# Reordering VectorE, ScalarE and POOL around the first two pairs of chunks in an output stage

## The chip, the cores and the metric

One core of a Trainium2 chip runs the whole program. The metric is the device time of one launch in microseconds. Five engines matter: TensorE (PE, with its weight loads shown apart as PEld), VectorE (DVE), ScalarE (ACT), GpSimd (POOL) and the DMA queues, most of them issued from SyncE (SP).

## The reference

The input x is 2048 by 448. The result is `g * a + (1 - g) * b`, with g a sigmoid gate of one number per row. Branch a is linear attention with 16 heads of width 28: q, k and v are projections of x, `phi(t) = where(t > 0, t + 1, exp(t)) + 1e-6` is applied to q and k, and then

```
kv  = einsum("bhsd,bhse->bhde", pk, v)
num = einsum("bhqd,bhde->bhqe", pq, kv)
den = einsum("bhqd,bhd->bhq", pq, z)[..., None] + 1e-6      # z: pk summed over the rows
a   = (num / den) @ wo
```

Branch b is a long convolution of x plus a skip; the kernel computes it with running sums when its taps are flat enough and with a general routine otherwise. With these inputs the general routine isn't entered.

## The kernel before, in words

The 2048 rows are 16 chunks of 128. A first stage goes over the chunks, projects k and q of each, and sums the outer product of pk and x into four PSUM banks g. fp32 products are made of fp32r pieces: an operand is split into a high part (ScalarE copies it, which rounds) and a low part (VectorE or POOL subtracts the high part), and three products of high and low parts are summed.

Between the stages (lines 716 to 821) the four banks are copied to SBUF as gs, multiplied by the v weights (`kv_products`), masked per head, split (kvh, kvl) and multiplied by wo. This gives a matrix M of 448 by 448, of which `m_high` and `m_low` write the parts mh and ml, four blocks of rows j. The q projection of the last chunk, 11 products, is spread over this stretch as filler for PE: `q_run(n)` issues the next n of them.

The output stage works on chunks in pairs. For chunk c:

- `norm_a(c)` on POOL multiplies pq by z into one of three buffers `prod`; `norm_b(c)` on DVE reduces it per head into the PSUM tile `den`.
- `norm_d(c, n)` finishes n chunks: a DVE multiply (L605), a DVE reciprocal (L607), and a copy of the result to SBUF for POOL (L610), on ACT where it says `ACT.copy`.
- `norm_c(c)` scales pq by that: POOL (L621), DVE (L624), POOL (L628), into `room`.
- `turn_pe(c)` transposes it on PE (L633) into a PSUM bank, t0 for the even chunk of a pair, t1 for the odd one.
- `turn_even` splits t0: ACT writes the high part th (L640), DVE the low part tl (L641). `odd_high` and `odd_low` do so for t1 (L652, L659). The odd chunk's fourth block lies in the even chunk's bank: `odd_ends(c, i, t0)` copies it on ACT (L656, two copies each) out of partitions 0 to 63 of t0 (i = 0) and 64 to 127 (i = 1).
- `attend(c)` is 11 products of 448 columns on PE (L676) in the order high, low, high and so on: the first loads th[c] block 2, the second tl[c] block 2, the sixth multiplies ml block 0, the ninth ml block 1, and the last two the ends.
- `final_b(c)` on DVE adds the gated convolution to it (L681) and the row block is written out from SP; `final_c(c)` copies it on ACT (L687).

The order of every engine's queue is that of the program text: the tile pools are under `manual_schedule()`, so an engine runs its instructions in the order in which the Python lines issue them, and waits are put in where an instruction touches a tile that another engine touched before. Each engine works through its queue strictly from the front; only PE's weight loads stand beside its products.

What the steps of the prediction touch: the kv products (L755), the M rows (L739, L743), the copies of the ends of M (L810, L813, L820), the first pair's lines 797 to 821, and the loop's turn c = 2 at lines 845 to 871.

Of the kernel before, what the change touches and what calls it, by code (L numbers as in the profile page):

```python
# [7 lines left out]
F32 = mybir.dt.float32  # L8
# [3 lines left out]
ALU = mybir.AluOpType  # L12
# [10 lines left out]
J = 4  # L23
# [119 lines left out]
def gated_mix_kernel(ctx: ExitStack, tc: tile.TileContext, xin, wq_d, wvo_d, abc_d, ldt_d, dsk_d,  # L143
                     turn_d, cst_d, first_d, gin_d, out):
    nc = tc.nc
    PE, ACT, DVE, POOL, SP = nc.tensor, nc.scalar, nc.vector, nc.gpsimd, nc.sync
# [62 lines left out]
    o = 0  # L209
    for part in PARTS:  # L210
# [8 lines left out]
        o = e  # L219
# [102 lines left out]
    def pieces(c, wh, wl, n, tag, last=None):  # L322
        o = ps.tile([P, 512], F32, name=tag, tag=tag)
        h, l = ([xt[c][:, i + k * P:i + (k + 1) * P] for k in range(J)] for i in (0, NAT))
        hh, lh, hl = ([(a[k], w[:, k]) for k in range(J)] for a, w in ((h, wh), (l, wh), (h, wl)))
        hl = hl[1:]
        if last == "x":
            seq = hh + hl + lh
        else:
            seq = [p for k in range(J) for p in (hh[k], lh[k])] + hl  # L330
            if last and len(last) > 1:
                seq = [{"h": hh, "l": lh, "w": [None] + hl}[i[0]][int(i[1])] for i in last.split()]
            elif last == "w":
                seq = seq[2:6] + seq[8:9] + seq[6:8] + seq[9:] + seq[:2]

        def run(count):
            for _ in range(min(count, len(seq))):
                a, b = seq.pop(0)
                run.n += 1
                PE.matmul(o[:, :n], lhsT=a, rhs=b, start=run.n == 1, stop=not seq)  # L340
        run.n = 0
        return o, run
# [249 lines left out]
    pn, th, tl, pd, dn, dp = {}, {}, {}, {}, {}, []  # L592

    def norm_a(c):
        pd[c] = prod[:, c % 3]
        POOL.tensor_tensor(out=pd[c], in0=pq[:, c], in1=zb, op=ALU.mult)  # L596

    def norm_b(c):
        if not dp:
            dp.append(ps.tile([P, 512], F32, name="den", tag="v1")[:, :NC * H].rearrange("p (c h) -> p c h", c=NC))  # L600
        DVE.tensor_reduce(out=dp[0][:, c], in_=pd.pop(c).rearrange("p (h d) -> p h d", h=H), op=ALU.add, axis=AX.X)  # L601

    def norm_d(c, n, copy=DVE.tensor_copy):
        r = dp[0][:, c:c + n]
        DVE.scalar_tensor_tensor(out=r, in0=r, scalar=1e-6, in1=e1[:, c:c + n, None].to_broadcast([P, n, H]),  # L605
                                 op0=ALU.add, op1=ALU.mult)
        DVE.reciprocal(out=r, in_=r)  # L607
        if c % 2 == 0:
            dn[c // 2] = tp.tile([P, 4, H], F32, name="den", tag="den", bufs=3)
        copy(dn[c // 2][:, c % 2:c % 2 + n], r)  # L610
# [5 lines left out]
    def norm_c(c):  # L616
        n = pn[c] = rf[:, c % 4 * NAT:][:, :NAT].rearrange("p (j t) -> p j t", j=J)
        r = dn[c // 2][:, c % 2]
        a = pq[:, c, :3 * DJ].rearrange("p (j h d) -> p j h d", j=3, h=4)
        b = pq[:, c, 3 * DJ:].rearrange("p (h d) -> p h d", h=4)  # L620
        POOL.tensor_tensor(out=n[:, :3, :DJ].rearrange("p j (h d) -> p j h d", h=4), in0=a,  # L621
                           in1=r[:, :H - 4].rearrange("p (j h) -> p j h", j=3)[:, :, :, None].to_broadcast([P, 3, 4, DH]),
                           op=ALU.mult)
        DVE.tensor_tensor(out=n[:, :3, DJ:].rearrange("p j (h d) -> p h j d", h=4),  # L624
                          in0=b[:, :, :DS].rearrange("p h (j d) -> p h j d", j=3),
                          in1=dp[0][:, c, H - 4:, None, None].to_broadcast([P, 4, 3, DS // 3]), op=ALU.mult)
        ends = pn[c // 2 * 2][:, 3, c % 2 * DT:][:, :DT].rearrange("p (h d) -> p h d", h=4)
        POOL.tensor_tensor(out=ends, in0=b[:, :, DS:], in1=r[:, H - 4:, None].to_broadcast([P, 4, DH - DS]), op=ALU.mult)  # L628

    def turn_pe(c):  # L630
        o = p3.tile([P, 512], F32, name="tr", tag="tr")
        for j in range(4 - c % 2):
            PE.transpose(o[:, j * P:(j + 1) * P], pn[c][:, j], ident)  # L633
        return o

    def turn_even(c, o):
        t = xt_p.tile([P, 2, J, P], F32R, name="th", tag="t")
        th[c], tl[c] = t[:, 0], t[:, 1]
        ov = o.rearrange("p (j t) -> p j t", j=J)
        ACT.copy(th[c], ov)  # L640
        DVE.tensor_tensor(out=tl[c], in0=ov, in1=th[c].bitcast(F32), op=ALU.subtract)  # L641

    def turn_odd(c, o, oe):
        odd_high(c, o)
        odd_ends(c, 0, oe)
        odd_ends(c, 1, oe)
        odd_low(c, o)

    def odd_high(c, o):
        t = xt_p.tile([P, 2, J, P], F32R, name="th", tag="t")  # L650
        th[c], tl[c] = t[:, 0], t[:, 1]
        ACT.copy(th[c][:, :3], o[:, :3 * P].rearrange("p (j t) -> p j t", j=3))  # L652

    def odd_ends(c, i, oe):
        for half in (slice(0, DT), slice(DT, P)):
            ACT.copy((th, tl)[i][c][half, 3], oe[i * DT:(i + 1) * DT, 3 * P:])  # L656

    def odd_low(c, o):
        DVE.tensor_tensor(out=tl[c][:, :3], in0=o[:, :3 * P].rearrange("p (j t) -> p j t", j=3),  # L659
                          in1=th[c][:, :3].bitcast(F32), op=ALU.subtract)  # L660
# [4 lines left out]
    def attend(c, cuts):  # L665
        av[c] = []
        even = c // 2 * 2
        h, l, ends = th[c], tl[c], (th, tl)[c % 2][even + 1][:, 3]
        for i, (lo, hi) in enumerate(cuts):
            pool, tag = ((p3, "a"), (p3, "a"), (ps, "v0"), (ps, "k"))[(c + i) % 4]  # L670
            a = pool.tile([P, 512], F32, name="a", tag=tag)
            av[c].append((a, lo, hi))
            seq = [(u_[:, j], w_[:, j]) for j in (2, 0, 1) for u_, w_ in ((h, mh), (l, mh), (h, ml))]
            seq += [(ends, mh[:, 3]), (tl[even][:, 3], low_w3[c % 2])]
            for n, (u_, w_) in enumerate(seq):
                PE.matmul(a[:, lo:hi], lhsT=u_, rhs=w_[:, lo:hi], start=n == 0, stop=n == 10)  # L676

    def final_b(c):
        ot = tp.tile([P, D], F32, name="ot", tag="pkh")
        for a, lo, hi in av[c]:  # L680
            DVE.scalar_tensor_tensor(out=ot[:, lo:hi], in0=y[:, c, lo:hi], scalar=og[:, c:c + 1],  # L681
                                     in1=a[:, lo:hi], op0=ALU.mult, op1=ALU.add)
            (ACT if c == NC - 1 and hi == D else SP).dma_start(out=oview[c, :, lo:hi], in_=ot[:, lo:hi])

    def final_c(c):
        for a, lo, hi in av.pop(c):
            ACT.copy(pq[:, c, lo:hi], a[:, lo:hi])  # L687

    c = NC - 2
# [26 lines left out]
    for i in range(4):  # L716
        do_g(c + 1, (i,))
        ACT.copy(gs[i], g[i][:, :D])
        if i == 1:
            qo, q_run = pieces(c + 1, wqh, wql, D + 2, "q")  # L720
# [17 lines left out]
    def m_high(j, o):  # L738
        ACT.copy(mh[:DJ, j] if j < 3 else shl[:, 0], o[:DJ, :D])  # L739
# [10 lines left out]
    def kv_products(r):  # L750
        kvp = ps.tile([P, 512], F32, name="k", tag="k") if r else p3.tile([P, 512], F32, name="tr", tag="tr")
        for j in (2 * r, 2 * r + 1):
            js = slice(j * DJ, (j + 1) * DJ)
            for k in range(4):
                PE.matmul(kvp[:DJ, js], lhsT=wv[:, (k + 1) % 4, js], rhs=gs[k][:, js], start=k == 0, stop=k == 3)  # L755
        return kvp
# [17 lines left out]
    def kv_low(r, o):  # L774
        DVE.tensor_tensor(out=kvl[:, 2 * r:2 * r + 2], in0=o, in1=kvh[:, 2 * r:2 * r + 2].bitcast(F32), op=ALU.subtract)

    q_run(1)
    k1 = kv_products(1)
    k0 = kv_products(0)
    k1 = kv_split(1, k1)  # L780
# [16 lines left out]
    t0 = turn_pe(0)  # L797
    t1 = turn_pe(1)
    q_run(2)
    norm_a(4)  # L800
    turn_even(0, t0)
    odd_high(1, t1)
    norm_b(2)
    norm_b(3)
# [2 lines left out]
    o1 = m_products(1, ps, "v0")  # L807
    m_high(0, o0)
    m_high(1, o1)
    ACT.copy(mh[:DT, 3], shl[:DT, 0].bitcast(F32))  # L810
    odd_ends(1, 0, t0)
    norm_d(2, 2, ACT.copy)
    ACT.copy(low_w3[0][:DT], shl[:DT, 0].bitcast(F32))  # L813
    m_low(0, o0)
    m_low(1, o1)
# [25 lines left out]
    norm_b(4)  # L841
    norm_a(7)
    norm_b(5)
    norm_d(4, 2, ACT.copy)
    for c in range(2, NC, 2):
        more = c + 2 < NC
        final_b(c - 2)
        t0 = turn_pe(c)
        t1 = turn_pe(c + 1)
        if more:  # L850
            norm_c(c + 2)
        if c + 6 < NC:
            norm_a(c + 6)
        if c + 4 < NC:
            norm_b(c + 4)
        turn_even(c, t0)
        if more:
            norm_c(c + 3)
        if c + 6 < NC:
            norm_a(c + 7)  # L860
        turn_odd(c + 1, t1, t0)
        final_c(c - 2)
        attend(c - 1, ((0, D),))
        if c + 4 < NC:
            norm_b(c + 5)
            norm_d(c + 4, 2, ACT.copy)
        final_b(c - 1)
        final_c(c - 1)
        attend(c, ((0, D),))
        for _ in range({4: 1, 6: 2}.get(c, 0)):  # L870
            next(later, None)
# [92 lines left out]
```

## Time and profile before

| | |
|---|---|
| time, median of 3 runs | 168.16 us (168.1 to 168.77) |
| the profiled execution's own time | 168.38 us |
| its span | 166.4 us |
| PE busy | 161.1 us (97%) |
| PEld busy | 144.9 us (87%) |
| DVE busy | 116.1 us (70%) |
| ACT busy | 109.4 us (66%) |
| POOL busy | 104.9 us (63%) |

The span is that of the program's instructions; some 2 us lie around it. A PE product of 448 columns is recorded as about 0.36 us, but products overlap in the array, so the distance between two starts is the number that adds up. The stretch of the change goes from about 112 us (kv products) over 118 to 126 us (first pair) to 130 us (the pair of c = 2).

### The profile page before, as it was taken

What the parts mean: (1) busy time and instruction counts of PE and PEld (TensorE: products, weight loads), DVE (VectorE), ACT (ScalarE), POOL (GpSimd) and SP (SyncE); (2) the same over time, 40 slices, a digit from 0 to 9 for tenths busy, and PEclk for the clock granted to TensorE, in tenths of its full rate; (3) what the DMA queues carried; (4) which work ended last, traced back from release to release, by engine and by line L of the source; (5) the groups of instructions that cost most, each with busy time, mean ns of one, the idle gap of its engine ahead of it and who ended that gap; (6) DMA issues with size and microseconds to landing.
All of it is one profiled execution on the core that took longest, in us unless ns stands there. A gap on an engine that the chain in (4) does not pass through costs nothing.

```text
span 166.4 us, 2609 instructions
## 1 busy us (share of the span) xinstructions
PE 161.1 (97%) x835; PEld 144.9 (87%) x835; DVE 116.1 (70%) x243; ACT 109.4 (66%) x257; POOL 104.9 (63%) x116
## 2 busy tenths in 40 slices
PE   6999999999999999999999999999999999999991
PEld 2698999999999999999999999988987999999990
DVE  0837753685852879889885555898899979986441
ACT  3688668988486784766758966453856766676541
POOL 3073589678809449477295999749689998633000
PEclk9999999999999999999999999999999999999998
DMA  5999966687974330959988007997121221122222
GB/s 157 411 314 321 287 143 230 228 295 276 336 255 136 126 107 19 221 141 250 295 261 165 0 4 117 185 203 161 27 46 55 110 110 55 61 110 110 110 78 95
DMA packets 10783, 27.51 MB, mean 165 GB/s; under 512 B 1328, under 2 KB 6992, under 8 KB 10544
## 3 DMA queue, kind: packets, MB, share of 16 engines
q1 hardware_dynamic: 8992, 21.71, 39.1%
q0 software_dynamic: 1632, 5.51, 17.6%
q8 instruction: 7, 0.11, 0.3%
q10 hardware_dynamic: 144, 0.11, 0.2%
q14 instruction: 8, 0.07, 0.1%
HBM read 17.87 MB, written 3.67 MB: 129 GB/s over the span
## 4 chain that ended last, share of the span: by engine, by line
PE 87%; DVE 6%; DMA 2%; ACT 1%; issue 1%; ACTq 0%; DVEq 0%
PE g L416 21%; PE q L340 19%; PE a L676 19%; PE v L340 12%; PE k L340 11%; PE tr L633 3%; DMA y<-in 2%; DVE den L601 2%; PE k L755 1%; DVE wk L743 1%; DVE th L641 1%; DVE ot L681 1%; ACT kvh L772 0%; DVE shl L743 0%; ACT wk L466 0%
## 5 line engine op out<-in xcount | busy, mean ns | idle before, releaser
L676 PE MATMUL a<-wk,th 128*128 128x448 f32 (+1 forms) x178 | 37.4, 357 | 0.3 <-DVE th L641 0.3
L416 PE MATMUL g<-pkh,xn 128*128 128x448 f32 x112 | 35.7, 364 | 0.0
L676 PEld LDWEIGHTS a<-wk,th 128*128 128x128 f32 x178 | 31.3, 188 | 2.9 <-DVE th L641 0.7
L237 POOL TENSOR_TENSOR xt<-xr,xt 128x512 fp32r<-128x512 f32 x14 | 18.2, 1298 | 19.8 <-ACT xt L241 19.8
L340 PE MATMUL q<-wqh,xt 128*128 128x450 f32 x120 | 27.8, 367 | 0.0
L237 POOL TENSOR_TENSOR xn<-xr,xn 128x448 fp32r<-128x448 f32 x16 | 19.6, 1228 | 10.1 <-ACT xn L247 10.1
L340 PEld LDWEIGHTS q<-wqh,xt 128*128 128x128 f32 x120 | 22.5, 189 | 1.8
L416 PE MATMUL g<-pkl,xn 128*128 128x448 f32 x64 | 23.3, 364 | 0.0
L416 PEld LDWEIGHTS g<-pkh,xn 128*128 128x128 f32 x112 | 21.1, 188 | 2.3
L596 POOL TENSOR_TENSOR prod<-pq,zb 128x448 f32<-128x448 f32 x16 | 18.3, 1154 | 4.5 <-ACT zb L709 2.9
L253 POOL TENSOR_TENSOR y<-xr,dsk 128x448 f32<-128x448 f32 x16 | 20.4, 1281 | 0.0
L340 PE MATMUL k<-wk,xt 128*128 128x448 f32 x88 | 19.7, 366 | 0.1
L340 PE MATMUL v<-wk,xt 128*128 128x448 f32 x88 | 18.9, 362 | 0.0
L340 PEld LDWEIGHTS k<-wk,xt 128*128 128x128 f32 x88 | 16.4, 188 | 2.0 <-ACT wk L466 0.5
L340 PEld LDWEIGHTS v<-wk,xt 128*128 128x128 f32 x88 | 16.5, 188 | 1.1
L681 DVE SCALAR_TENSOR_TENSOR ot<-y,og,a 128x448 f32<-128x448 f32 (+1 forms) x17 | 10.7, 626 | 7.5 <-PE a L676 7.3
L621 POOL TENSOR_TENSOR room<-pq,den 128x336 f32<-128x336 f32 x16 | 12.1, 756 | 5.4 <-issue 2.6
L687 ACT COPY pq<-a 128x448 f32<-128x448 f32 (+1 forms) x17 | 8.6, 512 | 5.8 <-DVE ot L681 5.6
L416 PEld LDWEIGHTS g<-pkl,xn 128*128 128x128 f32 x64 | 11.2, 174 | 1.1 <-DVE pkl L379 0.2
L656 ACT CAST th<-tr 64x128 fp32r<-64x128 f32 x32 | 8.3, 261 | 5.5 <-DVE th L641 5.1
L340 PE MATMUL q<-wql,xt 128*128 128x450 f32 x45 | 11.7, 366 | 0.0
L369 DVE SCALAR_TENSOR_TENSOR k<-k,e 128x448 f32<-128x448 f32 x8 | 5.1, 632 | 9.0 <-ACT e L368 8.8
(155 smaller groups left out, 289.7 us busy)
## 6 DMA issues: line engine op xcount, KB each, us to landing
xr<-in SPq DMA_DIRECT2D x15, 512.0 KB, 3.9
out<-ot SPq DMA_DIRECT2D x15, 224.0 KB, 1.9
room<-in SPq DMA_DIRECT2D x3, 896.0 KB, 7.5
wvo<-in SPq DMA_DIRECT2D x2, 896.0 KB, 5.5
y<-wvo POOLq DMA_DIRECT2D x2, 896.0 KB, 8.2
y<-room POOLq DMA_DIRECT2D x2, 896.0 KB, 9.2
y<-over POOLq DMA_DIRECT2D x2, 896.0 KB, 9.5
y<-in SPq DMA_DIRECT2D x2, 480.0 KB, 4.7
```

The costliest lines, as they stand in the source:

```text
L237: eng.tensor_tensor(out=o, in0=r, in1=h.bitcast(F32), op=ALU.subtract)
L253: POOL.tensor_tensor(out=y[:, c], in0=plain[c][:, :D], in1=dsk, op=ALU.mult)
L340: PE.matmul(o[:, :n], lhsT=a, rhs=b, start=run.n == 1, stop=not seq)
L369: DVE.scalar_tensor_tensor(out=pks[c], in0=pks[c], scalar=1.0, in1=e, op0=ALU.add, op1=ALU.max)
L416: PE.matmul(g[i][:a.shape[1], :D], lhsT=a, rhs=b, start=c == 0 and n == 0, stop=c == NC - 1 and n == len(seq) - 1)
L596: POOL.tensor_tensor(out=pd[c], in0=pq[:, c], in1=zb, op=ALU.mult)
L621: POOL.tensor_tensor(out=n[:, :3, :DJ].rearrange("p j (h d) -> p j h d", h=4), in0=a, in1=r[:, :H - 4].rearrange("p (j h) -> p j h", j=3)[ ...
L633: PE.transpose(o[:, j * P:(j + 1) * P], pn[c][:, j], ident)
L656: ACT.copy((th, tl)[i][c][half, 3], oe[i * DT:(i + 1) * DT, 3 * P:])
L676: PE.matmul(a[:, lo:hi], lhsT=u_, rhs=w_[:, lo:hi], start=n == 0, stop=n == 10)
L681: DVE.scalar_tensor_tensor(out=ot[:, lo:hi], in0=y[:, c, lo:hi], scalar=og[:, c:c + 1], in1=a[:, lo:hi], op0=ALU.mult, op1=ALU.add)
L687: ACT.copy(pq[:, c, lo:hi], a[:, lo:hi])
```

## The change

`turn_even` is cut into `even_high` (the ACT copy) and `even_low` (the DVE subtraction), and `turn_odd` is written out where it was called. Then four things are moved:

- One more of the last chunk's q products is issued in front of the kv products (2 in place of 1); the last group, `q_run(11)`, issues what is left.
- First pair: `even_low(0)` goes from before `norm_b(2)` to after `odd_ends(1, 0, t0)`. `norm_d(2, 2)` goes from after `odd_ends(1, 0, t0)` to before the copy into `mh[:DT, 3]`.
- The turn c = 2: `even_high(2)`, `odd_high(3)`, `norm_d(4, 2)` and `even_low(2)` come right after the transposes, ahead of `final_b(0)`. `norm_d(4, 2)` stood before the loop.
- In the same turn `norm_c(5)` comes ahead of `norm_a(8)` and `norm_b(6)`.

The turns c > 2 keep their order. No instruction is added or dropped.

```diff
@@ -634,17 +634,16 @@
     def turn_even(c, o):
+        even_high(c, o)
+        even_low(c, o)
+
+    def even_high(c, o):
         t = xt_p.tile([P, 2, J, P], F32R, name="th", tag="t")
         th[c], tl[c] = t[:, 0], t[:, 1]
-        ov = o.rearrange("p (j t) -> p j t", j=J)
-        ACT.copy(th[c], ov)
-        DVE.tensor_tensor(out=tl[c], in0=ov, in1=th[c].bitcast(F32), op=ALU.subtract)
-
-    def turn_odd(c, o, oe):
-        odd_high(c, o)
-        odd_ends(c, 0, oe)
-        odd_ends(c, 1, oe)
-        odd_low(c, o)
+        ACT.copy(th[c], o.rearrange("p (j t) -> p j t", j=J))
+
+    def even_low(c, o):
+        DVE.tensor_tensor(out=tl[c], in0=o.rearrange("p (j t) -> p j t", j=J), in1=th[c].bitcast(F32), op=ALU.subtract)
@@ -774,7 +773,7 @@
-    q_run(1)
+    q_run(2)
     k1 = kv_products(1)
@@ -798,7 +797,7 @@
     norm_a(4)
-    turn_even(0, t0)
+    even_high(0, t0)
     odd_high(1, t1)
     norm_b(2)
     norm_b(3)
@@ -807,9 +806,10 @@
     m_high(0, o0)
     m_high(1, o1)
+    norm_d(2, 2, ACT.copy)
     ACT.copy(mh[:DT, 3], shl[:DT, 0].bitcast(F32))
     odd_ends(1, 0, t0)
-    norm_d(2, 2, ACT.copy)
+    even_low(0, t0)
     ACT.copy(low_w3[0][:DT], shl[:DT, 0].bitcast(F32))
     m_low(0, o0)
     m_low(1, o1)
@@ -841,24 +841,34 @@
     norm_b(5)
-    norm_d(4, 2, ACT.copy)
     for c in range(2, NC, 2):
         more = c + 2 < NC
-        final_b(c - 2)
         t0 = turn_pe(c)
         t1 = turn_pe(c + 1)
+        if c == 2:
+            even_high(c, t0)
+            odd_high(c + 1, t1)
+            norm_d(c + 2, 2, ACT.copy)
+            even_low(c, t0)
+        final_b(c - 2)
         if more:
             norm_c(c + 2)
+        if c == 2:
+            norm_c(c + 3)
         if c + 6 < NC:
             norm_a(c + 6)
         if c + 4 < NC:
             norm_b(c + 4)
-        turn_even(c, t0)
-        if more:
-            norm_c(c + 3)
+        if c > 2:
+            turn_even(c, t0)
+            odd_high(c + 1, t1)
+            if more:
+                norm_c(c + 3)
         if c + 6 < NC:
             norm_a(c + 7)
-        turn_odd(c + 1, t1, t0)
+        for i in range(2):
+            odd_ends(c + 1, i, t0)
+        odd_low(c + 1, t1)
         final_c(c - 2)
         attend(c - 1, ((0, D),))
```

## Rows read from the trace of the kernel before

**Rows 1.** The page, parts 1 and 4: busy time by engine; chain by engine.
```profile
PE 161.1 (97%) x835; PEld 144.9 (87%) x835; DVE 116.1 (70%) x243; ACT 109.4 (66%) x257; POOL 104.9 (63%) x116
...
PE 87%; DVE 6%; DMA 2%; ACT 1%; issue 1%; ACTq 0%; DVEq 0%
```
**Rows 2.** Chain in order of time: start us, us, what it went through.
```profile
126.33 0.60 DVE th L641
...
155.99 6.88 PE a L676 x44
```
**Rows 3.** Timeline of PE: start us, us, instruction, count [idle before <-releaser].
```profile
120.83 2.39 PE L676 MATMUL a<-wk,th 128*128 128x448 f32 x11
123.06 1.15 PE L633 MATMUL tr<-both,room 128*128 128x128 f32 x7
...
126.26 0.37 PE L676 MATMUL a<-wk,th 128*128 128x448 f32 x1
...
129.08 0.93 PE L633 MATMUL tr<-both,room 128*128 128x128 f32 x7
...
132.06 2.38 PE L676 MATMUL a<-wk,th 128*128 128x448 f32 x11
```
**Rows 4.** Timeline of PE's weight loads, the transposes of chunk 2.
```profile
123.55 0.42 PEld L633 LDWEIGHTS tr<-both,room 128*128 128x128 f32 x4 [0.25 <-POOL room L628]
```
**Rows 5.** Timeline of DVE from the first pair to the third.
```profile
118.56 0.68 DVE L641 TENSOR_TENSOR th<-tr,th 128x512 fp32r<-128x512 f32 x1
119.16 1.35 DVE L601 TENSOR_REDUCE den<-prod 128x16 f32<-128x448 f32 x2
...
120.78 0.37 DVE L607 RECIPROCAL den<-den 128x32 f32<-128x32 f32 x1
121.05 1.14 DVE L743 TENSOR_TENSOR wk<-m,wk 112x448 fp32r<-112x448 f32 x2
...
122.69 0.19 DVE L624 TENSOR_TENSOR room<-pq,den 128x48 f32<-128x48 f32 x1
...
124.88 0.61 DVE L681 SCALAR_TENSOR_TENSOR ot<-y,og,a 128x448 f32<-128x448 f32 x1
...
126.24 0.68 DVE L641 TENSOR_TENSOR th<-tr,th 128x512 fp32r<-128x512 f32 x1
...
130.72 0.68 DVE L641 TENSOR_TENSOR th<-tr,th 128x512 fp32r<-128x512 f32 x1
```
**Rows 6.** Timeline of ACT in the first pair and the turn c = 2.
```profile
119.21 1.14 ACT L739 CAST wk<-m 112x448 fp32r<-112x448 f32 x2 [0.38 <-PE m L735]
120.25 0.56 ACT L810 CAST wk<-shl 64x448 fp32r<-64x448 f32 x1
120.71 0.53 ACT L656 CAST th<-tr 64x128 fp32r<-64x128 f32 x2
121.27 0.19 ACT L610 COPY den<-den 128x32 f32<-128x32 f32 x1
121.35 0.57 ACT L813 CAST wk<-shl 64x448 fp32r<-64x448 f32 x1
...
126.95 1.09 ACT L656 CAST th<-tr 64x128 fp32r<-64x128 f32 x4 [0.89 <-DVE th L641]
```
**Rows 7.** Timeline of all engines in the first stage, chunk 13's k.
```profile
93.08 0.55 ACT L373 ACTIVATE pkh<-v 128x448 fp32r<-128x448 f32 x1 [0.24 <-DVE v L369]
...
93.66 0.62 DVE L379 SCALAR_TENSOR_TENSOR zb<-v,zb 128x448 f32<-128x448 f32 x1 [0.61 <-ACT pkh L373]
```
**Rows 8.** Timeline of PE at the kv products.
```profile
112.38 2.19 PE L755 MATMUL k<-gs,wvo 128*112 128x112 f32 x16
114.41 1.74 PE L755 MATMUL tr<-gs,wvo 128*112 128x112 f32 x16
115.92 0.65 PE L735 MATMUL m<-wo,kvh 112*112 112x448 f32 x2
```
**Rows 9.** Timeline of PE's weight loads at the kv products.
```profile
113.34 1.06 PEld L755 LDWEIGHTS k<-gs,wvo 128*112 128x112 f32 x10 [0.16 <-ACT gs L718]
```
**Rows 10.** Timeline of POOL, the scaling of chunks 2 and 3 begins.
```profile
121.53 0.76 POOL L621 TENSOR_TENSOR room<-pq,den 128x336 f32<-128x336 f32 x1 [0.52 <-ACT den L610]
```
**Rows 11.** Stretches: busy us (x) of PE, PEld, DVE, ACT, POOL, granted clock, DMA, GB/s.
```profile
160.00:166.40 6.40, 2.85 (x25) 2.64 (x23) 1.58 (x3) 1.13 (x3) 0.00 (x0) 0.92 0.28 99
```

## The prediction

> **What bounds the kernel now.** I read the page first: PE is busy for 97% of the span, and the chain that ended last is 87% PE and 6% DVE [rows 1]. So time is won or lost where PE stands still, or where it does something it needn't; no work is dropped here, so only standing still counts. The chain in order of time comes next, to find where it leaves PE: its last DVE piece is the low part of chunk 2 at 126.33 us, and from there it is PE up to the last 44 products [rows 2]. Whatever PE gains or loses before 127 us therefore arrives at the end undiminished, as long as the other engines keep up. Third, the PE timeline over the first two pairs, read by starts. Eleven products take 123.06 - 120.83 = 2.23 us (0.203 each). Seven transposes and an attend take 132.06 - 129.08 = 2.98 in an undisturbed turn, but 126.26 - 123.06 = 3.20 in the first: 0.22 lost, where a transpose waited for POOL's scaling of chunk 3 [rows 3, 4]. The attend of chunk 2 takes 129.08 - 126.26 = 2.82, so 0.59 is lost, to the low part on DVE that ended at 126.24 + 0.68 = 126.92 [rows 3, 5]. These 0.81 us are all that the two pairs have to give. Last, DVE and ACT in the same stretch, because their queues are what is reordered.
>
> **Part 1, one more q product in front of the kv products.** The first 16 kv products take 114.41 - 112.38 = 2.03 us and the next 16 take 1.51 [rows 8]; the 0.52 between them is waiting for the copies gs, the last of which releases PE at 113.34 [rows 9]. A product of 0.20 put in front pushes the first pairs into that wait, and the release at 113.34 stays. I cost it at nothing there, and it shortens the last q group by 0.20, so the first attend could begin at 120.63. If the cover failed, the kv chain and everything behind it would be 0.20 later: the bounds are -0.20 and +0.20. What it really gives depends on part 2.
>
> **Part 2, the first pair.** Taken from 118.56, the low part of chunk 0 frees 119.16 - 118.56 = 0.60 us of DVE: the two reductions start at 118.56, and the reciprocal ends at 120.78 + 0.37 - 0.60 = 120.55 [rows 5]. POOL's scaling, which waited for the copy of that result, could begin 0.68 earlier than 121.53 (copy at 120.59 in place of 121.27), and release the transposes at 123.55 - 0.68 = 122.87; the 0.22 stall goes [rows 4, 6, 10].
>
> The question is when the low part itself now runs. By its place in DVE's queue it would follow the reciprocal at once, at 121.05 - 0.60 = 120.45. But it now comes, in program order, after `odd_ends(1, 0, t0)`, and both read the same PSUM bank, on two engines. Does a second reader wait for the first? In the first stage DVE's `zb<-v,zb` needs nothing that ACT's `pkh<-v` writes, only the bank v that both read; it stands idle for 0.61 us and starts at 93.66, 0.03 after ACT's end at 93.63 [rows 7]. The other way round, in this very bank: the ends copies of the turn c = 2 wait 0.89 us and start at 126.95, when the low part of chunk 2 has ended at 126.92, though they use nothing of it [rows 5, 6]. So readers on two engines are kept in program order, and DVE will wait for ACT here.
>
> The Trainium skill ("PSUM — Partial Sum Buffer", section "PSUM bank collisions raise a hardware error") says that two engines must not be in the same bank and quadrant of partitions at once, reads included, and that the hardware does not stall for it, so software must. By its quadrants the two would still meet in partitions 0 to 63 and the sum stands; by the other sentence taken alone, an order that no semaphore enforced, it would be the first rival's sum. The trace agrees with the former: both waits above are there, 0.61 and 0.89 us.
>
> ACT's side, in its new order: the two M copies end at 119.21 + 1.14 = 120.35; the copy of the reciprocal waits for DVE until about 120.59; the copy into mh follows 0.08 later (121.35 - 121.27), at 120.67; the ends 0.46 later (120.71 - 120.25), at 121.13, and they end 0.53 later, at 121.66 [rows 6]. DVE, idle since 120.55, starts the low part at 121.70 and ends it at 122.38. Behind it in DVE's queue stand the two low parts of M, now at 121.70 + 0.60 = 122.30 and not 121.05: the whole DVE queue is 1.25 later [rows 5].
>
> PE: the first attend starts at 120.63, its second product needs that low part. How an attend goes on after such a wait is in the trace: the low part of chunk 2 ended at 126.92 and that attend at 129.08, 2.16 later [rows 3, 5]. So this one ends at 122.38 + 2.16 = 124.54, against 123.06: 1.48 later. The 0.20 of part 1 disappears in this wait. The low parts of M, at 122.91 and 123.44, are in time for the sixth and ninth product (about 123.3 and 123.9), and DVE's last piece of chunk 3's scaling (122.69 + 0.19 + 1.25 = 124.13) is 0.4 ahead of the transposes.
>
> **Part 3, the turn c = 2.** Transposes and attend of chunk 1, undisturbed: 124.54 + 2.98 = 127.52. The low part of chunk 2 now stands before `final_b(0)`, a scaling piece and `norm_b(6)`, which took 126.24 - 124.88 = 1.36 [rows 5]; it runs at 124.88 + 1.25 = 126.13 and ends at 126.81, 0.7 ahead of need. The 0.59 stall goes. Attend of chunk 2: 127.52 + 2.23 = 129.75, against 129.08. **Net +0.67.** The same as 1.48 - 0.22 - 0.59.
>
> **Part 4, what DVE owes afterwards.** The 1.36 us moved behind the low part of chunk 2 have to be done before that of chunk 4: 126.13 + (130.72 - 126.24) + 1.36 = 131.97, ended at 132.65. The load for the second product of that attend is due about 132.06 + 0.67 = 132.73 [rows 3, 5]. It fits with 0.08 us to spare, where it had 132.06 - 131.40 = 0.66. POOL's scaling of chunks 4 and 5 begins after the reciprocal, and that too is up to 1.25 later where PE is 0.67 later; the transposes at 129.08 show no wait. Once this pair is through, the debt shrinks, as DVE waits for each attend of PE. I take nothing, and keep +0.3 as the other end.
>
> **The sum.** The profiled execution took 168.38, so it would take 169.05. It lies 0.22 above the median 168.16; carried to the median: 168.83. A change within 0.5%, 0.84 us, can't be told from none.
>
> **Rivals.**
> 1. *DVE does not wait for the ends copies.* Then the low part runs at 120.45 and ends at 121.13; the first attend ends at 121.13 + 2.16 = 123.29, the second at 126.27, and the low part of chunk 2, ready at 125.56, leaves attend 2 to end at 128.50: 0.58 earlier, 167.6. It decides at one place, the start of L641 in the first pair: before 121.1 and the kernel is faster, after that each 0.1 costs 0.1. For it speaks only that the ends copies read a quarter of the columns and half of the partitions; against it, two waits of just this kind. 8%.
> 2. *DVE's debt reaches PE at chunk 4*, or the q product in front is not hidden. Either adds 0.2 to 0.3: 169.0 to 169.2. For it speaks the thin margin; against it, that most of the reordered work is paid by then, and the gs wait of 0.52. 18%.
> 3. *The clock falls.* PE would stand still for about 1.6 us in the first attend, against 0.59 now [rows 3]. In this trace it dropped after the last product: the last stretch has 2.85 us of PE and a mean grant of 0.92, so about 1.0 of its 6.4 us were at 1.2 GHz and the drop came some 2.5 us after PE's end [rows 11]. At 1.2 GHz the products would take twice 0.20 for as long as it lasts; an attend or two would add 2.2 to 4.4 us: 171 or more. 3%. The Trainium skill ("TensorE: Matmul & The Clock Gate", section "What's actually happening") says that the clock falls after idleness; the trace agrees, and only with an idle time longer than this one.
> 4. *The order is not what the text says.* The trace follows the text line by line on DVE and ACT [rows 5, 6], so under 1%.
>
> **How the numbers follow.** Forecast 71%: 168.5 to 169.1 by itself, since the ACT chain of six instructions is summed from starts that may differ by 0.2. Range 168.2 to 169.4: it takes in the second rival and 0.3 below the forecast; out are the first rival, the clock and some tails. Faster by over 0.5% (below 167.32) needs the first rival and more: 5%, with what I overlooked. Slower by over 0.5% (above 169.00): a fifth of the forecast, the second rival's greater part and the clock, 27%. Within: 68%.
>
> **What would show it.** L641 of the first pair starting at 121.7, just after L656, with an idle DVE ahead of it; the second product of the first attend released by L641 at 122.4; no POOL release at the transposes of chunk 3; no release by L641 in chunk 2's attend; chunk 4's low part ending less than 0.3 us before its load. A start of L641 at 120.5 would overturn the forecast, and so would kv products ending after 114.5.

## The result and the profile after

The changed kernel takes 169.05 us (median of 15 runs, 168.64 to 169.44) against 168.37 for the kernel before on the same chips (15 runs): a ratio of 1.0038, 95% interval 1.0024 to 1.0053. That is 0.64 us slower, where the forecast said 0.67 (168.83 from the median then known). In the profiled execution (168.71 us, span 166.9) PE is busy a little less and is more of the chain, DVE less:

```profile
PE 160.5 (96%) x835; PEld 145.0 (87%) x835; DVE 116.1 (70%) x243; ACT 109.5 (66%) x257; POOL 104.9 (63%) x116
...
PE 92%; DVE 3%; ACT 2%; issue 0%; ACTq 0%; POOL 0%; DVEq 0%; POOLq 0%
```

Against [rows 1], ACT's share of the chain has gone from 1% to 2%. Where it stands, the chain in order of time shows (start, us, what it went through):

```profile
119.86 0.38 DVE den L607
...
120.26 0.19 ACT den L610
120.44 0.46 ACT wk L810
120.91 0.16 ACT th L655
...
121.08 0.27 ACT th L655
...
121.37 0.70 DVE th L646
```

Read it downwards: the reciprocal on DVE, its copy on ACT, the copy into mh, the two ends copies, and only then DVE again with the low part of chunk 0 (L646 in the new text; L655 are the ends copies). The same on DVE's own timeline, which answers to [rows 5]:

```profile
118.24 1.35 DVE L601 TENSOR_REDUCE den<-prod 128x16 f32<-128x448 f32 x2
...
119.86 0.37 DVE L607 RECIPROCAL den<-den 128x32 f32<-128x32 f32 x1
121.37 0.69 DVE L646 TENSOR_TENSOR th<-tr,th 128x512 fp32r<-128x512 f32 x1 [1.14 <-ACT th L655]
121.98 1.14 DVE L742 TENSOR_TENSOR wk<-m,wk 112x448 fp32r<-112x448 f32 x2
...
125.81 0.67 DVE L646 TENSOR_TENSOR th<-tr,th 128x512 fp32r<-128x512 f32 x1
...
131.51 0.68 DVE L646 TENSOR_TENSOR th<-tr,th 128x512 fp32r<-128x512 f32 x1
```

DVE is idle for 1.14 us and is released by the ends copies. ACT over the same stretch, which answers to [rows 6]:

```profile
118.89 1.15 ACT L738 CAST wk<-m 112x448 fp32r<-112x448 f32 x2 [0.37 <-PE m L734]
120.26 0.19 ACT L610 COPY den<-den 128x32 f32<-128x32 f32 x1 [0.21 <-DVE den L607]
120.34 0.56 ACT L810 CAST wk<-shl 64x448 fp32r<-64x448 f32 x1
120.81 0.53 ACT L655 CAST th<-tr 64x128 fp32r<-64x128 f32 x2
```

And PE, which answers to [rows 3] and [rows 8]:

```profile
112.27 1.99 PE L754 MATMUL k<-gs,wvo 128*112 128x112 f32 x16
114.09 1.74 PE L754 MATMUL tr<-gs,wvo 128*112 128x112 f32 x16
...
120.34 0.41 PE L675 MATMUL a<-wk,th 128*128 128x448 f32 x1
122.11 2.27 PE L675 MATMUL a<-wk,th 128*128 128x448 f32 x10 [1.36 <-DVE th L646]
124.22 0.93 PE L633 MATMUL tr<-both,room 128*128 128x128 f32 x7
...
127.19 2.37 PE L675 MATMUL a<-wk,th 128*128 128x448 f32 x11
129.41 0.93 PE L633 MATMUL tr<-both,room 128*128 128x128 f32 x7
...
132.37 2.37 PE L675 MATMUL a<-wk,th 128*128 128x448 f32 x11
...
162.88 0.28 PE L675 MATMUL a<-ends,th 128*128 128x224 f32 x1
```

The load of the second product's weights shows the same wait, from the end of the load before it:

```profile
122.11 1.90 PEld L675 LDWEIGHTS a<-wk,th 128*128 128x128 f32 x10 [1.65 <-DVE th L646]
```

The first attend is one product, a gap, and ten products. After that PE runs without a break: transposes and attend of chunk 1 in 127.19 - 124.22 = 2.97 us, attend of chunk 2 in 2.22, both at their undisturbed size. The two stalls of before are gone, one larger one has come.

**How to compare two traces here.** The stages before the change differ by some tenths of a microsecond between executions, as the second 16 kv products show: 114.09 here, 114.41 before. So I compare a distance D: from the start of the first kv product to the start of the last product on PE, with 0.20 added where the extra q product stands ahead of the first. Before: 162.57 - 112.38 = 50.19. After: 162.88 - 112.27 + 0.20 = 50.81. The difference, 0.62, is what the change did between the two. Each D comes from one profiled execution and has no interval. e7 and e9 below, which are the same kernel, differ by 0.31, nearly all of it in one late transfer.

### The profile page after: what moved, and what is told of

Its sections match the earlier page's. It is cut to its first block, busy times and chain, and to the rows that moved or that the text cites. A ratio compares the mean times of both kernels' runs of the same rounds, so it can differ in the third digit from the quotient of the medians.

```text
span 166.9 us, 2611 instructions
## 1 busy us (share of the span) xinstructions
PE 160.5 (96%) x835; PEld 145.0 (87%) x835; DVE 116.1 (70%) x243; ACT 109.5 (66%) x257; POOL 104.9 (63%) x116
## 4 chain that ended last, share of the span: by engine, by line
PE 92%; DVE 3%; ACT 2%; issue 0%; ACTq 0%; POOL 0%; DVEq 0%; POOLq 0%
PE a L675 21%; PE g L416 21%; PE q L340 19%; PE v L340 12%; PE k L340 11%; PE tr L633 3%; PE q L259 3%; PE k L754 1%; DVE den L601 1%; ACT kvh L771 0%; DVE th L646 0%; DVE wk L742 0%; DVE shl L742 0%; POOL warm L193 0%; ACT wk L810 0%
## 5 line engine op out<-in xcount | busy, mean ns | idle before, releaser
L655 ACT CAST th<-tr 64x128 fp32r<-64x128 f32 x32 | 8.3, 260 | 5.0 <-DVE th L646 4.6
```

## Experiments

The theory, W: two engines that read the same PSUM bank are kept in the order of the program text, so the low part of chunk 0 waits for the ends copies. Rivals: Q, the new order of the queues is itself what costs; T, the reordered turn c = 2 is what costs. D and the measured ratio of each kernel (95% interval):

| kernel | D, us | against before | ratio to before |
|---|---|---|---|
| before | 50.19 | | |
| changed | 50.81 | +0.62 | 1.0038 (1.0024 to 1.0053) |
| e1 low part issued first | 49.58 | -0.61 | 0.9965 (0.9947 to 0.9983) |
| e2 copy back | 50.42 | +0.23 | 1.0019 (1.0004 to 1.0033) |
| e3 first pair alone | 51.44 | +1.25 | 1.0087 (1.0063 to 1.0111) |
| e4 turn c = 2 alone | 49.64 | -0.55 | 0.9983 (0.9967 to 0.9998) |
| e5 front product alone | 50.18 | -0.01 | 1.0017 (1.0001 to 1.0034) |
| e6 e1, order in attend 0 | 49.44 | -0.75 | 0.9952 (0.9935 to 0.9969) |
| e7 e6, both turns | 51.65 | +1.46 | 1.0026 (1.0011 to 1.0041) |
| e8 low part in two | 50.73 | +0.54 | 1.0023 (1.0001 to 1.0044) |
| e9 e7 again | 51.96 | +1.77 | 1.0027 (0.9998 to 1.0056) |

**e1, the same queues, the other order between them.**

```diff
     norm_d(2, 2, ACT.copy)
+    even_low(0, t0)
     ACT.copy(mh[:DT, 3], shl[:DT, 0].bitcast(F32))
     odd_ends(1, 0, t0)
-    even_low(0, t0)
```

> The changed kernel with even_low(0) issued ahead of the copy into mh and of odd_ends(1, 0), so that every engine's queue holds the same instructions in the same order as in the changed kernel; only who waits for whom is turned round. Theory W (DVE's low part waits for ACT's ends copies because both read the bank t0 and the ends come first in program order): the low part starts right after the reciprocal, about 0.6 us after the reciprocal's start is 0.3, not 1.5; the first attend ends about 1.25 us earlier, and the time is 0.58 us below the kernel before (ratio 0.9965), 1.25 below the changed kernel. Rival Q (the new order of the queues themselves costs, the low part standing behind two reductions, a multiply and a reciprocal): no change against the changed kernel, ratio 1.004.

DVE's timeline in e1:

```profile
120.31 0.37 DVE L607 RECIPROCAL den<-den 128x32 f32<-128x32 f32 x1
120.59 0.67 DVE L646 TENSOR_TENSOR th<-tr,th 128x512 fp32r<-128x512 f32 x1
```

PE's weight loads in e1:

```profile
121.31 1.91 PEld L675 LDWEIGHTS a<-wk,th 128*128 128x128 f32 x10 [0.40 <-DVE th L646]
```

No idle time on DVE, 0.28 us from the reciprocal's start to the low part's, and the weight load's wait in the first attend down from 1.65 to 0.40. Every queue holds what it held in the changed kernel, so Q falls. The ratio, 0.9965, is the one expected, and is also what the prediction's first rival worked out for a DVE that does not wait (-0.58).

**e2, a dose of the same wait.** The ends copies come 0.4 us earlier on ACT, since the copy that waits for the reciprocal stands behind them.

```diff
+    late_copy = []
-    norm_d(2, 2, ACT.copy)
+    norm_d(2, 2, lambda o, r: late_copy.append((o, r)))
     ACT.copy(mh[:DT, 3], shl[:DT, 0].bitcast(F32))
     odd_ends(1, 0, t0)
+    ACT.copy(*late_copy[0])
     even_low(0, t0)
```

> The changed kernel with the ACT copy of norm_d(2, 2) put back behind the ends copies, its two DVE instructions left where they are. Theory W: the ends copies no longer wait for the reciprocal and end about 0.42 us earlier, so the low part starts 0.42 us earlier and so does everything behind it: ratio to the kernel before about 1.0015 (0.25 us slower), the low part idle for about 0.7 us ahead of it and not 1.14. Rival Q: the low part keeps its place in DVE's queue and its time, ratio 1.004.

DVE in e2, then ACT in e2:

```profile
120.89 0.69 DVE L646 TENSOR_TENSOR th<-tr,th 128x512 fp32r<-128x512 f32 x1 [0.73 <-ACT th L655]
```

```profile
120.32 0.53 ACT L655 CAST th<-tr 64x128 fp32r<-64x128 f32 x2
120.88 0.19 ACT L813 COPY den<-den 128x32 f32<-128x32 f32 x1
```

The wait is 0.73 and not 1.14, D is +0.23 and not +0.62: what the ends copies give, 0.41, arrives at the end as 0.39. The interval of the timed ratio, 1.0004 to 1.0033, takes in W's 1.0015 and leaves out Q's 1.004.

**e3 and e4, the two parts apart.** e3 is the kernel before with

```diff
-    turn_even(0, t0)
+    even_high(0, t0)
...
+    norm_d(2, 2, ACT.copy)
     ACT.copy(mh[:DT, 3], shl[:DT, 0].bitcast(F32))
     odd_ends(1, 0, t0)
-    norm_d(2, 2, ACT.copy)
+    even_low(0, t0)
```

and e4 the kernel before with the loop of the changed one.

> The kernel before with the first pair's part of the change alone: even_low(0) behind odd_ends(1, 0), norm_d(2, 2) ahead of the copy into mh; one q product in front and the turn c = 2 as before. Theory W: DVE's queue is 1.25 us later from the low part on and nothing makes it up, so the low part of chunk 2 is 1.25 later and the attend of chunk 2 waits for it still: 1.25 us slower than the kernel before, ratio 1.0074. Rival T (the turn c = 2 is what costs, and the first pair costs little): ratio below 1.002.

> The kernel before with the reordered turn c = 2 alone. By the prediction's part 3: the low part of chunk 2 runs 1.36 us earlier, at 124.9, before it is needed; the stall of 0.59 us in that attend goes and the time is 0.59 below the kernel before, ratio 0.9965. The low part of chunk 4 is then due some 0.6 us earlier and not itself earlier, so up to 0.1 of it may be given back. Rival T (the turn costs): ratio at or above 1.

PE's weight loads in e3:

```profile
122.50 1.90 PEld L675 LDWEIGHTS a<-wk,th 128*128 128x128 f32 x10 [1.61 <-DVE th L646]
...
128.30 1.91 PEld L675 LDWEIGHTS a<-wk,th 128*128 128x128 f32 x10 [0.72 <-DVE th L646]
```

The first wait is new, the second is that of chunk 2 as before: DVE is late for both, and nothing is made up. D is +1.25, as expected; the ratio, 1.0087, is 1.46 us, with an interval of 1.06 to 1.87. PE and DVE in e4:

```profile
126.19 2.38 PE L675 MATMUL a<-wk,th 128*128 128x448 f32 x11
128.40 0.93 PE L633 MATMUL tr<-both,room 128*128 128x128 f32 x7
```

```profile
124.80 0.67 DVE L646 TENSOR_TENSOR th<-tr,th 128x512 fp32r<-128x512 f32 x1
```

The low part of chunk 2 ends at 125.47, 0.7 ahead of the attend, which takes 2.21 and no longer 2.82. So T falls: the turn gains 0.55 in the trace. The timed ratio gives 0.28 us, with an interval of 0.03 to 0.56, at the edge of the trace's number. In D the parts add up: 1.25 - 0.55 = 0.70, against 0.62 for both. By the timed ratios the sum is 1.46 - 0.28 = 1.18 us, against 0.64, so the timed runs bear this out less closely.

**e5, the q product.** The kernel before with `q_run(2)` in front.

> The kernel before with one more q product in front of the kv products and nothing else. By the prediction's part 1 it hides in the wait for the copies gs: the 16 kv products take 1.8 us in place of 2.03, the second 16 start where they did. The first attend may begin some 0.1 to 0.2 us earlier, then waits the longer for POOL at the transposes and for DVE in the attend of chunk 2, so nothing of it arrives: ratio 1.000 within the noise. Rival (not hidden): 0.20 us slower, ratio 1.0012, with the second 16 kv products 0.2 later behind the copies.

PE and its weight loads in e5:

```profile
112.84 1.98 PE L754 MATMUL k<-gs,wvo 128*112 128x112 f32 x16
114.66 1.54 PE L754 MATMUL tr<-gs,wvo 128*112 128x112 f32 x14
```

```profile
123.82 0.42 PEld L633 LDWEIGHTS tr<-both,room 128*128 128x128 f32 x4 [0.28 <-POOL room L628]
...
127.21 1.90 PEld L675 LDWEIGHTS a<-wk,th 128*128 128x128 f32 x10 [0.69 <-DVE th L646]
```

The second 16 kv products follow 1.82 us after the first, not 2.03, so the product is hidden; the waits for POOL and DVE are as before, and D is unchanged. The timed ratio is 1.0017, with an interval that just leaves out 1. No line of this trace after 112 us holds those 0.3 us. Its first `v` product began at 8.35, 0.30 later than in the profile of before, at a place that the edit doesn't touch (the last section has more on this); whether the timed runs differ in that way isn't shown, so where the 0.3 us come from stays open.

**e6, more of the first attend's wait.** e1, and

```diff
             seq = [(u_[:, j], w_[:, j]) for j in (2, 0, 1) for u_, w_ in ((h, mh), (l, mh), (h, ml))]
+            if c == 0:
+                seq = [seq[k] for k in (0, 2, 3, 1, 4, 5, 6, 7, 8)]
```

> e1_low_issued_first, and in the attend of chunk 0 the products with the low part of x one place later: high part with mh, high part with ml, high part of the next block, then the low part. Theory W says that what is left of the first attend's wait is for the low part (0.4 us in e1); it shrinks by about 0.3. The low part of chunk 4 ends at 131.4 in e1, and its load is then due at 131.3: part of the gain goes there, by the prediction's part 4. Ratio to the kernel before 0.995 to 0.9965, not clearly below e1; in the trace a wait by the low part of chunk 4 that e1 has not. If DVE's debt is no matter (rival), the full 0.9 us: 0.9946.

PE's weight loads at chunk 4 in e6, and DVE:

```profile
130.95 2.19 PEld L677 LDWEIGHTS a<-wk,th 128*128 128x128 f32 x11
```

```profile
130.42 0.68 DVE L646 TENSOR_TENSOR th<-tr,th 128x512 fp32r<-128x512 f32 x1
```

This is the fastest kernel of the study: 167.61 us, ratio 0.9952, below the kernel before and the changed one. It isn't clearly below e1: D falls by 0.14 against e1, about half of the 0.3 by which the first attend's wait was to shrink, and the intervals of the two ratios overlap. The wait that I expected at chunk 4 isn't there: the low part ends at 131.10, the load is due at 131.15. Nothing is left over, but nothing is lost.

**e7 and e9, the same idea one turn further.** e6, with the high and low parts of chunk 4 ahead of `final_b(2)`.

```diff
-        if c == 2:
+        if c < 5:
             even_high(c, t0)
             odd_high(c + 1, t1)
-            norm_d(c + 2, 2, ACT.copy)
+            if c == 2:
+                norm_d(c + 2, 2, ACT.copy)
             even_low(c, t0)
```

> e6_attend0_order, and in the turn c = 4 too the high and low part of the even chunk come ahead of final_b. If the wait in e6 is DVE's debt, it goes: 0.9 us below the kernel before, ratio 0.9947, and no weight load waits for a low part from 122 us on.

It is 1.28 us slower than e6 by the medians (168.89 and 167.61), and my expectation was wrong. The profiled execution was also an unusual one (169.84), with a transfer that took 3.7 us to land, so the same kernel was run again as e9.

> e7_both_turns once more, because its profiled execution had a transfer that landed 1.3 us later than in any other profile and so can't show where the rest of its 1.2 us over e6 comes from. Theory: ahead of final_b the low part of chunk 4 waits for ACT's high part, DVE stands idle for about a microsecond in a stretch where it has none to spare, and the debt comes out as waits of PE for low parts of chunks 4 to 8, about 1.2 us together. Rival: the late transfer is the cause and comes back in this profile, with no PE wait for a low part.

e9, DVE and then PE's weight loads:

```profile
131.98 0.69 DVE L646 TENSOR_TENSOR th<-tr,th 128x512 fp32r<-128x512 f32 x1 [1.09 <-ACT th L643]
```

```profile
124.74 0.30 PEld L677 LDWEIGHTS a<-wk,th 128*128 128x128 f32 x2 [1.78 <-ACT ends L822]
...
138.83 1.90 PEld L677 LDWEIGHTS a<-wk,th 128*128 128x128 f32 x10 [0.24 <-DVE th L646]
...
144.75 1.91 PEld L677 LDWEIGHTS a<-wk,th 128*128 128x128 f32 x10 [0.84 <-DVE th L646]
```

The page of e9, its row for the attends' products (busy us, mean ns, idle us before and what ended most of it):

```profile
L677 PE MATMUL a<-wk,th 128*128 128x448 f32 (+1 forms) x178 | 38.0, 359 | 1.9 <-DMA wk<-shl 1.4
```

Two things at once. Moved ahead of `final_b(2)`, the low part of chunk 4 waits 1.09 us for ACT's high part, with work that could have filled the time queued behind it; DVE is that much later, and PE waits for low parts at chunks 6 and 8, 0.24 and 0.84 us. That is the theory, and both profiles show it. But the late transfer came back as well. A weight load of the first attend stood for 1.78 us, which the view puts down to ACT, though that ACT copy had ended 1.0 us before; the page puts 1.4 us of PE's idle time down to the transfer. So the rival isn't out. Both profiled executions, 169.84 and 170.61, lie above the medians, 168.89 and 169.02, by 0.95 and 1.59 us, and the wait was 1.50 us in e7 and 1.78 in e9. How the 1.28 us of the typical run divides between the two stays open.

**e8, by bank or by columns?**

```diff
-    even_low(0, t0)
+    for cols in (slice(0, 3), slice(3, 4)):
+        DVE.tensor_tensor(out=tl[0][:, cols], in0=t0.rearrange("p (j t) -> p j t", j=J)[:, cols],
+                          in1=th[0][:, cols].bitcast(F32), op=ALU.subtract)
```

> The changed kernel with the low part of chunk 0 cut in two, blocks 0 to 2 (384 columns) first and block 3 behind it; the ends copies read block 3 alone. If readers are kept in order by bank, the first piece still waits for the ends copies, DVE idle about 1.1 us ahead of it, and the time is the changed kernel's or 0.1 us above it (ratio to the kernel before 1.004). If they are kept in order by the columns that both read, the first piece runs right after the reciprocal, the first attend's wait shrinks from 1.4 to about 0.3 us, but block 3's piece still waits for the ends copies and the two low parts of M stand behind it: the time falls by about 0.6 us at most against the changed kernel (ratio 1.000).

DVE in e8:

```profile
121.74 0.76 DVE L813 TENSOR_TENSOR th<-tr,th 128x384 fp32r<-128x384 f32 x2 [1.14 <-ACT th L655]
```

The first piece reads columns 0 to 383 and the ends copies columns 384 to 511; it still waits 1.14 us. So the order isn't kept by columns. It is kept by the bank or by the tile t0; the tile fills its bank here, so this run can't tell the two apart. The timed ratio, 1.0023 (1.0001 to 1.0044), hardly tells the two expectations apart; the wait does. The Trainium skill ("PSUM — Partial Sum Buffer", section "PSUM bank collisions raise a hardware error") says that two engines still collide when they access different columns of one bank in the same quadrant of partitions. The run shows the wait of 1.14 us, not what would happen without it, which wasn't tried.

## Why the prediction was right

Step by step, with 0.31 us taken off the forecast's clock (the kv products, counted as for D, began so much earlier in this execution):

| step of the prediction | forecast - 0.31 | trace |
|---|---|---|
| first attend begins | 120.32 | 120.34 |
| low part of chunk 0 starts | 121.39 | 121.37 |
| second product released | 122.1 | 122.11 |
| transposes of chunk 2 | 124.23 | 124.22 |
| low part of chunk 2 starts | 125.82 | 125.81 |
| attend of chunk 2 ends | 129.44 | 129.41 |
| low part of chunk 4 ends | 132.34 | 132.19 |
| total | +0.67 | +0.62 |

- *Part 1.* Right: hidden at the kv products, swallowed afterwards (e5).
- *Part 2.* This decided it. Without the wait the step would have been -0.58, and e1 measures -0.61 for exactly that. The two rows on which the reading stood [rows 6, 7] were enough; e8 adds that it doesn't go by columns.
- *Part 3.* Right: the stalls of 0.22 and 0.59 are gone in the trace, and e4 measures the latter alone as 0.55.
- *Part 4.* Too pessimistic by 0.15 us. The two `final_b` took 1.39 us before, as the second waited for PE, and take 1.19 when DVE is late. The margin at chunk 4 was about 0.2 and not 0.08, and the debt cost nothing at chunk 4, not even in e6, where PE comes to that place earlier still. A later wait for a low part shows in e4, 0.18 us at chunk 8. Part 4 didn't enter the sum.
- *The clock.* It held through the gap: the granted clock is 1.00 (2.4 GHz) in every stretch from 118 to 160 us. Behind the gap, transposes with an attend take 2.97 us and an attend alone 2.22, as before.
- *A slip in rival 1.* By its own terms, 0.68 + 2.16 + 2.98 + 2.23 = 8.05 us from the start of the low part to the end of chunk 2's attend, the kernel breaks even at a start of 129.08 - 8.05 = 121.03, not 121.1. Nothing hung on it.

The single steps agree to a few hundredths of a microsecond up to the attend of chunk 2, so the total isn't right by luck.

So the change pairs a good move (the turn c = 2, -0.55) with a costly one (the first pair, +1.25). With the low part issued two lines higher, as in e1, the first pair no longer costs. That its move would then gain something of its own isn't shown: e1 lies only 0.06 below e4 in D, and the intervals of their ratios overlap.

## What to carry to other kernels

When an instruction is moved in the text, look not only at its own queue but at what it now comes after on other engines: two readers of one PSUM bank were kept in the order of the text here, though neither uses what the other writes, and the later one inherits the whole queue in front of the earlier. Which of two such readers is issued first is free to choose, and in e1 it was worth 1.2 us with every queue unchanged. And an instruction that feeds PE is worth moving forward only as far as its own inputs are ready: past that point it idles its engine (1.09 us of DVE in e9, though what this cost in time isn't separated there from the late transfer).

## What the runs showed of the hardware that I had not expected

A transfer may have been held up by the fetch of instructions. The 112 KB transfer into mh landed in 2.2 or 2.3 us in nine of the eleven profiles; in e7 it took 3.7 and in e9 4.0, and PE waited. The DMA view of e9, 116 to 126 us:

```profile
wk<-shl SPq DMA_DIRECT2D x1, 112.0 KB, 4.0
```

The view of 121.9 to 124.7 us has an instruction packet in the transfer's time:

```profile
q8 instruction: 1, 0.02, 3.3%
```

The same view of e6, 119.9 to 122.2 us, has none beside the transfer:

```profile
q1 hardware_dynamic: 182, 0.23, 47.0%
...
wk<-shl SPq DMA_DIRECT2D x1, 112.0 KB, 2.2
```

In e6 that packet comes after 122.5, when the transfer has landed. The packet takes 3.3% of 16 engines over 2.8 us, that is 1.5 us of one engine; the transfer is 1.8 us late. In e9 the transfer's queue has no packet at all between 122.9 and 123.4 us and only five after that. That the packet is the cause is read from the coincidence in both profiles of that kernel, not tested; why it came earlier there, I can't say.

The start of the program explains most of what the profiled executions differ by ahead of the change. The first `v` product began anywhere from 7.70 to 8.51 us in the eleven profiles, and the first kv product, counted as for D, always 104.26 to 104.35 us after it. Among the first products, a filler of 512 columns took 0.39 us in the profile of before and still 0.65 at 6.56 us in that of e9, and the first `v` products began at 8.05 and 8.51. Why they differ isn't shown. PE timelines, before and then e9:

```profile
5.70 0.39 PE L259 MATMUL q<-warm 128*128 128x512 bf16 x1
...
8.05 0.37 PE L340 MATMUL v<-wk,xt 128*128 128x448 f32 x1
```

```profile
6.56 0.65 PE L259 MATMUL q<-warm 128*128 128x512 bf16 x1
...
8.51 0.76 PE L340 MATMUL v<-wk,xt 128*128 128x448 f32 x3
```

Such a difference is as large as the effects measured here, which is why D and not the span was compared.
